# RWKV-6 attention and an MLP mixer on one core: the first channel weights' loads moved behind the third unit's last product, and their conversion moved with them

## The chip, the cores and the metric

The kernel runs on one core of one Trainium2 chip. The metric is the device time of one execution in microseconds. A core has TensorE (PE; its weight loads are listed as PEld), VectorE (DVE), ScalarE (ACT), GpSimd (POOL) and SyncE (SP), which here issues nearly all DMAs. Each engine takes its instructions in the order of its own queue.

## The reference, cut to what matters

Four batches, 8 heads, 768 tokens, 48 features a head (so 384 columns). First a linear attention with a decaying state, then a mixer over tokens and over channels:

```python
for t in range(S):
    cur = einsum('bhd,bhe->bhde', u * k[t], v[t])
    y[t] = einsum('bhd,bhde->bhe', r[t], state + cur)
    state = w[t][..., None] * state + einsum('bhd,bhe->bhde', k[t], v[t])
x = y.transpose(0, 2, 1, 3).reshape(B, S, H * D)
h = maximum(x.T @ w_tok1, 0) @ w_tok2        # per batch, 768 -> 256 -> 768
u = x + h.T
out = u + maximum(u @ w_ch1, 0) @ w_ch2      # 384 -> 1536 -> 384
```

The four weight matrices are 64-bit floats in HBM; all else is 32-bit.

## The kernel before, in words

The attention of a batch is cut into three *units* of 256 tokens, `e0`, `e1`, `e2` for the first batch. A unit loads its decays, keys and queries, and values (`load_w` L158, `load_part` L166 and `load_rk` L170, `load_v` L177), scans the decays on DVE (`ends`, `begins`), scales keys and queries, builds products of keys and queries (`own_gram`, `gram`, L308), carries the state over the chunks (`outer` L356, `scaled` L492, `update` L499), and forms its output in PSUM from two sets of products: `across` (L371, called by `before`) and `within` (L392, called by `after`). `taken` (L398) copies it into `x`, which is tiled as 128 tokens x 384 columns, six chunks a batch. `ranges` (L418) are ACT passes that check the decays' range.

The mixer of the first batch (`mixing`) begins with the *hidden* products over tokens (L883; twelve, `h[0]` to `h[11]`), `rectified` (ACT, L886, two), the *back* products (L891; six chunks), an addition into `x` on DVE (L893), and *turns*, transposes on TensorE (L902) that ACT copies into `xT` (L904). Then comes the up-projection over channels (L926, rectified by ACT at L929) and the down-projection (L937). One product of 32-bit floats is run as two passes, each with its weight load.

The weights reach 32 bits by conversions of 1,024 values a partition each, three for the token weights (`to_tok`) and nine for the channel weights (`to_ch`). `convert` (L230) makes for each one these functions, in the order in which they are named at the unpacking: a load of two DMAs of 512 KB (L257), `exponent` (x, DVE, L260), `mantissa` (m, DVE, L266), `raise_two` (p, ACT, L263), `add` (DVE, L272), `signs` (g, ACT, L269) and `put`, which is two things on DVE: the factor times its sign (L275), and the scaled product into the weights' tile (L278). The raw bits of `to_ch[0]` go to tile `z0`, those of `to_ch[1]` and `to_ch[2]` to parts of tile `raw`.

The order of the work around the change is written out by hand: the call of `strict` that begins at L1024 lists the pieces, and every engine, SP's DMA queue included, takes its instructions in this order (`strict`, L103). `behind(gate, f)` (L94) adds a wait, so that `f` is not issued before the last instruction of `gate` is done. From there on an order string (`WEAVES`) merges `first_mixing`, the attention of the next batch and the remaining conversions; its first pieces are the back products, the `put` of `to_ch[0]` and the steps of `to_ch[1]`. In the DVE queue after the list stand: L275 and L278 for `to_ch[0]`, L260 for `to_ch[1]`, the first L893, L266, two more L893, L272, two more L893, L275, L278. In the ACT queue after the list: L269 for `to_ch[1]`, two steps of the next unit's `own_u` (L324), L263 for `to_ch[1]`, and the copies L904.

SP's DMAs in this place, in order: values of the third unit, the first load of `to_ch[0]` (two DMAs into `z0`, behind `h[2]`), the load of `to_ch[2]` (behind `add1`), the load of `to_ch[1]` (behind `e2`'s `before`), keys and queries of unit 3 (four DMAs of 192 KB, behind `e0`'s `after`), those of unit 4 (four more), and the load of `to_ch[3]`.

Of the kernel before, what the change touches and what calls it, by code (L numbers as in the profile page):

```python
# [17 lines left out]
ALU = mybir.AluOpType  # L18
# [7 lines left out]
UB = C // UC  # L26
# [39 lines left out]
def rwkv6_then_mixer(  # L66
# [18 lines left out]
    pe, dve, act, pool, sp = nc.tensor, nc.vector, nc.scalar, nc.gpsimd, nc.sync  # L85
# [8 lines left out]
    def behind(gate, f):  # L94

        def g():
            done = len(block.instructions)
            f()
            tc.add_manual_dep(block.instructions[done], ended[gate], wait, reason="time of issue")

        return g
# [61 lines left out]
    def rk_of(i):  # L163
        return rks[i if i < UB else (i - UB) % 2]

    def load_part(i, n):  # L166
        for rows in (slice(0, 128),) if i < UB else (slice(0, D), slice(P, P + D)):
            sp.dma_start(rk_of(i)[rows, ts(n, COLS)], rk[i, n, rows, :])

    def load_rk(i):  # L170
        if i < NU:
            for n in (1, 0):
                load_part(i, n)
# [3 lines left out]
    def load_v(i):  # L177
        if i < NU:
            vs[i] = vpool.tile([128, UC, DM], f32, name="vt", tag=f"vt{i % 2 if i < UB else 1}")
            b, j = divmod(i, UB)  # L180
            sp.dma_start(vs[i], v[b, ts(j, UC * 128), :].rearrange("(c p) e -> p c e", p=128))
# [48 lines left out]
    def convert(pair, raw, room, signs_at=None):  # L230

        d64 = bits64[raw]
        lo, hi = (d64.rearrange("p (n two) -> p n two", two=2)[:, :, j] for j in range(2))
        top = d64.bitcast(u16).rearrange("p (n four) -> p n four", four=4)[:, :, 3]
        m, planes = mantissas[room], exponents[room]
        mf, e, power = m.bitcast(f32), *planes[:2]
        sign, factor = planes[2 * room].bitcast(bf16) if signs_at is None else signs_at, power.bitcast(bf16)

        (a, _), (b, _) = pair
        c, k = a.shape[1:]  # L240
        (row, _), (one, _) = a.ap[1:]
        apart = b.offset - a.offset if a.tensor is b.tensor else None
        beside = apart == k * one
        if beside:
            whole = bass.AP(a.tensor, a.offset, [list(a.ap[0]), [row, c], [one, 2 * k]])
        elif apart is not None and (c == 1 or apart == c * row):
            whole = bass.AP(a.tensor, a.offset, [list(a.ap[0]), [apart // c, 2 * c], [one, k]])
        else:
            whole = None

        def load():
            for n, (dst, src) in enumerate(pair):
                if beside:
                    to = d64.rearrange("p (c n k) -> p n c k", n=2, c=c)[:, n]
                else:
                    to = d64[:, ts(n, 2 * PIECE)].rearrange("p (c k) -> p c k", c=dst.shape[1])
                sp.dma_start(to, src)  # L257

        def exponent():
            dve.tensor_scalar(e, top, 0x7FF0, None, op0=ALU.bitwise_and)  # L260

        def raise_two():
            act.activation(power, e, AF.Relu, bias=rebias, scale=8.0)  # L263

        def mantissa():
            dve.tensor_scalar(m, hi, 0xFFFFF, 0x100000, op0=ALU.bitwise_and, op1=ALU.bitwise_or)  # L266

        def signs():
            act.activation(sign, hi.bitcast(i32), AF.Sign)  # L269

        def add():
            dve.scalar_tensor_tensor(mf, lo, 2.0 ** -32, m, op0=ALU.mult, op1=ALU.add)  # L272

        def put():
            dve.tensor_mul(factor, factor, sign)  # L275
            for dst, cols in [(whole, slice(0, 2 * PIECE))] if whole is not None else [(dst, ts(n, PIECE)) for n, (dst, _) in enumerate(pair)]:
                x, by = (t[:, cols].rearrange("p (c k) -> p c k", c=dst.shape[1]) for t in (mf, factor))
                dve.scalar_tensor_tensor(dst, x, 2.0 ** -20, by, op0=ALU.mult, op1=ALU.mult)  # L278

        return load, exponent, mantissa, raise_two, add, signs, put  # L280

    def blocks(t, src, c, k):
# [5 lines left out]
    def conversion(*weights, rooms):  # L288
        pieces = [e for w in weights for e in blocks(*w)]
        return [convert(pieces[2 * n:2 * n + 2], *rooms(n)) for n in range(len(pieces) // 2)]  # L290
# [9 lines left out]
    def put(q, j):  # L300
        return ts(j ^ q, T)
# [703 lines left out]
    def interleaved(order, *streams):  # L1005
# [7 lines left out]
    h = [lambda i=i, c=c: turned["hidden"](i, c) for c in range(C) for i in range(DTOK // 128)]  # L1013
    rectified = [lambda i=i: turned["rectified"](i) for i in range(DTOK // 128)]
    bits64.append(turned["xT"].rearrange("p m t -> p (m t)").bitcast(u32)[:, :4 * PIECE])
    to_tok = conversion((wtok1, w_tok1, 2, 256), (wtok2, w_tok2, 2, 256), rooms=lambda n: (3, 0) if n == 2 else (n, n))
    to_ch = conversion((now["wch1"], w_ch1, 1, 512), (now["wch2"], w_ch2, 4, 128), rooms=lambda n: (n % 2, 0, rks[2][:, ts(n % 2, PIECE)].bitcast(bf16)) if n else (2, 1))
    e0, e1, e2 = (unit(i) for i in range(UB))
    (_, x0, m0, p0, add0, g0, put0), (_, x1, m1, p1, add1, g1, put1), (_, x2, m2, p2, add2, g2, put2) = to_tok
    _, x3, m3, p3, add3, g3, _ = to_ch[0]  # L1020
    in_turn.update({pe.engine: None, dve.engine: None, act.engine: None, sp.engine: None})
    s0, s1, s2 = (e["updates"] for e in (e0, e1, e2))
    t0, t1, t2 = (e["scaled"] for e in (e0, e1, e2))
# [6 lines left out]
           behind(t0[2], to_tok[1][0]), e1["copied"][1], t1[0], e1["carry"], e2["own_u"][2], s1[0], g0, e0["seen"], e1["own_put"], e2["own_u"][3],  # L1030
           t1[1], e0["after"], e1["queries"], s1[1], e0["taken"][0], e2["ends"], m0, lambda: load_w(3), e1["gram"], lambda: load_v(2), e2["keys"],
           m1, t1[2], behind(e0["carry"], to_tok[2][0]), s1[2], add0, e2["tokens"], add1, e0["taken"][1], e0["taken"][2], t1[3], e2["copied"][0],
           e2["copied"][1], s1[3], t2[0], e1["ranges"][0], g1, put0, e1["before"], e2["carry"], behind(e1["before"], lambda: load_part(2, 0)), h[0],
           s2[0], h[1], e1["mask"], x2, e2["begins"], e1["seen"], e1["after"], t2[1], p2, e1["taken"][0], s2[1], e2["own_gram"], x1, e2["queries"],
           t2[2], lambda: load_v(UB), h[3], e1["taken"][1], s2[2], e1["taken"][2], t2[3], e2["own_put"], h[2], p1, e2["gram"], e2["before"], g2, m2,
           behind(h[2], to_ch[0][0]), h[4], e2["mask"], put1, e2["seen"], add2, e2["after"], e2["ranges"][0], e2["taken"][0], x3, h[5], h[6],
           e2["taken"][1], e2["taken"][2], h[7], h[8], e1["ranges"][1], h[9], g3, m3, behind(add1, to_ch[2][0]), h[10], h[11], rectified[0],
           rectified[1], p3, behind(e2["before"], to_ch[1][0]), behind(e0["after"], lambda: load_rk(3)), e2["ranges"][1], put2, add3)

    six_banks.close()  # L1040
    ps_g, ps_m = None, six_banks.enter_context(tc.tile_pool(name="ps_m", bufs=6, space=bass.MemoryType.PSUM))
# [228 lines left out]
```

## Time and profile before

| what | value |
|---|---|
| median of 3 runs | 486.51 us (485.17 to 490.95) |
| the profiled execution | 487.42 us |
| its span in the trace | 485.7 us |
| mean granted TensorE clock | 0.997 |
| PE, DVE, ACT busy | 464.4, 340.0, 254.0 us |

The span goes from the first instruction to the last; the time of the execution has 1.7 us more around it. A row of the timeline reads: start, duration, engine, line, operation, output<-input, shape, number of instructions, and in brackets the idle time before it with what ended it. "issue" there is idle time in which the engine waited for nothing that the profile shows.

### The profile page before, as it was taken

The numbers are of one execution on the slowest core, as the hardware profiler recorded it, in microseconds if no ns is written. First come the engines' busy times: TensorE is split into PE (matmuls) and PEld (weight loads), VectorE is DVE, ScalarE is ACT, GpSimd is POOL, SyncE is SP. The second block draws the span as 40 slices with busy tenths as digits, with TensorE's granted clock in tenths as the row PEclk, the third lists the DMA queues.
The fourth block names the chain that finished last, engine by engine and source line by source line (L and its number), as shares of the span: only waits on it lengthen the run. The fifth ranks groups of instructions, "written<-read, shape, count | busy, mean of one in ns | idle before, by whom it ended". The sixth has DMA issues, their size and how long they took to land.

```text
span 485.7 us, 12678 instructions
## 1 busy us (share of the span) xinstructions
PE 464.4 (96%) x5298; PEld 406.2 (84%) x5298; DVE 340.0 (70%) x478; ACT 254.0 (52%) x587; POOL 62.7 (13%) x58
## 2 busy tenths in 40 slices
PE   2897999999999999999999999999999999999995
PEld 2775588866697668999999979999999979999995
DVE  7999699697796788868855388758977365235331
ACT  5887666745678666453564336344646334134140
POOL 1000000000000000313232003040403003032030
PEclk9999999999999999999999999999999999999998
DMA  8868545690385495856636662385724622436321
GB/s 300 295 206 306 142 151 188 209 303 34 111 246 174 131 242 177 258 170 205 212 112 216 224 195 84 132 220 180 227 85 133 223 84 81 112 102 197 91 86 55
DMA packets 49407, 83.77 MB, mean 172 GB/s; under 512 B 4864, under 2 KB 40576, under 8 KB 49344
## 3 DMA queue, kind: packets, MB, share of 16 engines
q1 hardware_dynamic: 49056, 82.80, 54.4%
q8 instruction: 43, 0.70, 0.6%
q14 instruction: 20, 0.16, 0.1%
q10 hardware_dynamic: 288, 0.10, 0.1%
HBM read 71.87 MB, written 11.01 MB: 171 GB/s over the span
## 4 chain that ended last, share of the span: by engine, by line
PE 91%; DVE 2%; issue 1%; ACT 0%; DVEq 0%
PE h_ps L937 10%; PE ends_ps L730 8%; PE ends_ps L737 8%; PE ends_ps L732 8%; PE o_ps L748 8%; PE o_ps L750 8%; PE o_ps L749 8%; PE z_ps L926 7%; PE h_ps L653 5%; PE z_ps L922 3%; PE h_ps L684 3%; PE gram L308 3%; PE y_ps L392 2%; PE y_ps L371 2%; PE kv_ps L356 2%; PE h_ps L883 2%
## 5 line engine op out<-in xcount | busy, mean ns | idle before, releaser
L723 POOL TENSOR_TENSOR z_high<-z_high 128x384 fp32r<-128x384 f32 x48 | 61.4, 1289 | 406.5 <-ACT before L492 208.8
L756 DVE SCALAR_TENSOR_TENSOR x<-o_ps,x 128x384 f32<-128x384 f32 x35 | 19.1, 557 | 50.5 <-PE o_ps L750 50.5
L712 ACT ACTIVATE z_high<-ends_ps 128x384 fp32r<-128x384 f32 x48 | 23.5, 489 | 52.3 <-PE ends_ps L737 51.7
L730 PE MATMUL ends_ps<-x_forms,forms 128*128 128x384 f32 x216 | 50.4, 341 | 0.0
L737 PE MATMUL ends_ps<-z_more,forms 128*128 128x384 f32 x216 | 50.3, 341 | 0.0
L732 PE MATMUL ends_ps<-x_forms,ring 128*128 128x384 f32 x216 | 49.3, 337 | 0.0
L719 DVE SCALAR_TENSOR_TENSOR z_high<-ends_ps,z_high 128x384 fp32r<-128x384 f32 x48 | 26.5, 553 | 32.0 <-ACT z_high L712 31.9
L937 PE MATMUL h_ps<-wch,z 128*128 128x384 f32 x144 | 48.5, 490 | 0.0
L748 PE MATMUL o_ps<-forms,z_high 128*128 128x384 f32 x140 | 48.1, 343 | 0.0
L749 PE MATMUL o_ps<-ring,z_high 128*128 128x384 f32 x140 | 47.1, 337 | 0.0
L750 PE MATMUL o_ps<-forms,z_high 128*128 128x384 f32 x140 | 47.1, 336 | 0.0
L492 ACT ACTIVATE before<-state,to_end 112x48 f32<-112x48 f32 x132 | 33.2, 324 | 22.3 <-DVE state L507 21.4
L937 PEld LDWEIGHTS h_ps<-wch,z 128*128 128x128 f32 x144 | 26.7, 190 | 17.0
L737 PEld LDWEIGHTS ends_ps<-z_more,forms 128*128 128x128 f32 x216 | 39.0, 188 | 0.3 <-DVE z_more L625 0.2
L730 PEld LDWEIGHTS ends_ps<-x_forms,forms 128*128 128x128 f32 x216 | 38.0, 188 | 0.7
L732 PEld LDWEIGHTS ends_ps<-x_forms,ring 128*128 128x128 f32 x216 | 38.5, 188 | 0.0
L926 PE MATMUL z_ps<-xT,wch 128*128 128x256 f32 x144 | 32.2, 381 | 0.0
L926 PEld LDWEIGHTS z_ps<-xT,wch 128*128 128x128 f32 x144 | 26.9, 190 | 3.7
L715 ACT ACTIVATE z_high<-z_high 128x384 fp32r<-128x384 f32 x48 | 25.2, 525 | 3.3
L748 PEld LDWEIGHTS o_ps<-forms,z_high 128*128 128x128 f32 x140 | 26.3, 188 | 0.2
L749 PEld LDWEIGHTS o_ps<-ring,z_high 128*128 128x128 f32 x140 | 26.3, 188 | 0.0
L750 PEld LDWEIGHTS o_ps<-forms,z_high 128*128 128x128 f32 x140 | 26.3, 188 | 0.0
(194 smaller groups left out, 931.9 us busy)
## 6 DMA issues: line engine op xcount, KB each, us to landing
ring<-third SPq DMA_DIRECT2D x144, 192.0 KB, 3.2
raw<-in_w_ch_dram SPq DMA_DIRECT2D x16, 512.0 KB, 5.0
rk<-in_rk_dram SPq DMA_DIRECT2D x36, 192.0 KB, 5.9
near<-in_near_dram SPq DMA_DIRECT2D x8, 768.0 KB, 4.6
w<-in_w_dram SPq DMA_DIRECT2D x10, 520.5 KB, 3.6
vt<-in_v_dram SPq DMA_DIRECT2D x12, 384.0 KB, 4.3
out_dram<-x SPq DMA_DIRECT2D x17, 192.0 KB, 3.4
third<-forms SPq DMA_DIRECT2D x12, 192.0 KB, 3.4
```

The source lines that it names most:

```text
L492: act.mul(t[:ROWS, a], state[bt, g][:ROWS, a], by_last(c, j)[:, a:a + 1])
L715: act.mul(z_form(jt, 2), z_form(jt, 0).bitcast(f32), 1.0 / BASE)
L719: dve.scalar_tensor_tensor(z_form(jt, 1), a, 0.0, z_form(jt, 0).bitcast(f32), op0=ALU.max, op1=ALU.subtract)
L723: pool.tensor_add(z_form(jt, 2), z_form(jt, 2).bitcast(f32), z_form(jt, 1).bitcast(f32))
L730: pe.matmul(a, up[m], xf[0][:, m], start=m == 0, stop=False)
L732: pe.matmul(a, low[:, m], xf[1][:, m], start=False, stop=False)
L737: pe.matmul(banks["a", jt], joint, xf[2][:, m], start=False, stop=m == 2)
L748: pe.matmul(a, z[0], up, start=first, stop=False, skip_group_check=True)
L749: pe.matmul(a, z[1], held[bt, s, half, 1, jt], start=False, stop=False, skip_group_check=True)
L750: pe.matmul(a, z[2], joint, start=False, stop=last, skip_group_check=True)
L926: pe.matmul(ps, now["wch1"][:, m, ts(jt, 128)], xT[:, m, ts(s, SEG)], start=(m == 0), stop=(m == DM // 128 - 1))
L937: pe.matmul(ps, zs[s][:, jt, ts(n, 128)], now["wch2"][:, jt, :], start=(jt == 0), stop=(jt == NJ - 1))
```

## The change

`put` is cut in two, so that its halves can be listed separately; for the three token conversions they are named `product0` and `put0` and so on, and both stay on DVE. In the list, three things move:

- the load of `to_ch[0]` is issued behind `e2`'s `after` (the last product of the third unit) instead of behind `h[2]`. The loads of `to_ch[2]`, `to_ch[1]` and of unit 3's rows are listed behind it, in the same order and with their own gates as before;
- `x3`, `m3`, `g3`, `p3` (the first channel conversion's steps on DVE and ACT) move to the end of the list, ahead of `add3`;
- `product2` and `put2` thereby come ahead of `x3` on DVE, and `rectified` and the range check `e2["ranges"][1]` ahead of `g3` on ACT.

On DVE the only difference in order is that L260 and L266 of `to_ch[0]` come behind L275 and L278 of the third token conversion (L272 follows as before). On ACT L269 of `to_ch[0]`, which stood ahead of both L886, comes behind them and behind L418, with L263 next to it. The order on SP, TensorE and GpSimd is the same. Lines of the changed kernel are 5 to 7 higher from L281 on.

```diff
-        def put():
-            dve.tensor_mul(factor, factor, sign)
+        def signed(on=dve):
+            on.tensor_tensor(factor, factor, sign, ALU.mult)
+
+        def put(whole_step=True):
+            if whole_step:
+                signed()
...
+        put.apart = lambda on: (lambda: signed(on), lambda: put(False))
...
+    (product0, put0), (product1, put1), (product2, put2) = (put.apart(on) for put, on in zip((put0, put1, put2), (dve, dve, dve)))
...
-           e2["copied"][1], s1[3], t2[0], e1["ranges"][0], g1, put0, e1["before"], ...
+           e2["copied"][1], s1[3], t2[0], e1["ranges"][0], g1, product0, put0, e1["before"], ...
...
-           ..., e2["gram"], e2["before"], g2, m2,
-           behind(h[2], to_ch[0][0]), h[4], e2["mask"], put1, e2["seen"], add2, e2["after"], e2["ranges"][0], e2["taken"][0], x3, h[5], h[6],
-           e2["taken"][1], e2["taken"][2], h[7], h[8], e1["ranges"][1], h[9], g3, m3, behind(add1, to_ch[2][0]), h[10], h[11], rectified[0],
-           rectified[1], p3, behind(e2["before"], to_ch[1][0]), behind(e0["after"], lambda: load_rk(3)), e2["ranges"][1], put2, add3)
+           ..., e2["gram"], e2["before"], g2, m2, h[4], e2["mask"], product1, put1, e2["seen"], add2, e2["after"],
+           behind(e2["after"], to_ch[0][0]), e2["ranges"][0], e2["taken"][0], h[5], h[6], e2["taken"][1], behind(add1, to_ch[2][0]),
+           behind(e2["before"], to_ch[1][0]), behind(e0["after"], lambda: load_rk(3)), e2["taken"][2], h[7], h[8], e1["ranges"][1], h[9], h[10],
+           h[11], rectified[0], rectified[1], e2["ranges"][1], product2, put2, x3, m3, g3, p3, add3)
```

More of the change, by code (lines that the diff above doesn't have):

```diff
@@ L1032, in rwkv6_then_mixer @@
            m1, t1[2], behind(e0["carry"], to_tok[2][0]), s1[2], add0, e2["tokens"], add1, e0["taken"][1], e0["taken"][2], t1[3], e2["copied"][0],
-           e2["copied"][1], s1[3], t2[0], e1["ranges"][0], g1, put0, e1["before"], e2["carry"], behind(e1["before"], lambda: load_part(2, 0)), h[0],
-           s2[0], h[1], e1["mask"], x2, e2["begins"], e1["seen"], e1["after"], t2[1], p2, e1["taken"][0], s2[1], e2["own_gram"], x1, e2["queries"],
-           t2[2], lambda: load_v(UB), h[3], e1["taken"][1], s2[2], e1["taken"][2], t2[3], e2["own_put"], h[2], p1, e2["gram"], e2["before"], g2, m2,
-           behind(h[2], to_ch[0][0]), h[4], e2["mask"], put1, e2["seen"], add2, e2["after"], e2["ranges"][0], e2["taken"][0], x3, h[5], h[6],
-           e2["taken"][1], e2["taken"][2], h[7], h[8], e1["ranges"][1], h[9], g3, m3, behind(add1, to_ch[2][0]), h[10], h[11], rectified[0],
-           rectified[1], p3, behind(e2["before"], to_ch[1][0]), behind(e0["after"], lambda: load_rk(3)), e2["ranges"][1], put2, add3)
+           e2["copied"][1], s1[3], t2[0], e1["ranges"][0], g1, product0, put0, e1["before"], e2["carry"],
+           behind(e1["before"], lambda: load_part(2, 0)), h[0], s2[0], h[1], e1["mask"], x2, e2["begins"], e1["seen"], e1["after"], t2[1], p2,
+           e1["taken"][0], s2[1], e2["own_gram"], x1, e2["queries"], t2[2], lambda: load_v(UB), h[3], e1["taken"][1], s2[2], e1["taken"][2], t2[3],
+           e2["own_put"], h[2], p1, e2["gram"], e2["before"], g2, m2, h[4], e2["mask"], product1, put1, e2["seen"], add2, e2["after"],
+           behind(e2["after"], to_ch[0][0]), e2["ranges"][0], e2["taken"][0], h[5], h[6], e2["taken"][1], behind(add1, to_ch[2][0]),
+           behind(e2["before"], to_ch[1][0]), behind(e0["after"], lambda: load_rk(3)), e2["taken"][2], h[7], h[8], e1["ranges"][1], h[9], h[10],
+           h[11], rectified[0], rectified[1], e2["ranges"][1], product2, put2, x3, m3, g3, p3, add3)
     six_banks.close()
```

## The prediction, on record before the changed kernel ran

> **What bounds the kernel now.** I read the page first. TensorE is busy for 96% of the span and carries 91% of the chain that ended last.
>
> ```profile
> span 485.7 us, 12678 instructions
> PE 464.4 (96%) x5298; PEld 406.2 (84%) x5298; DVE 340.0 (70%) x478; ACT 254.0 (52%) x587; POOL 62.7 (13%) x58
> PE 91%; DVE 2%; issue 1%; ACT 0%; DVEq 0%
> ```
>
> Then the table by stage, for the place of the change (about 38 to 61 us) and for all that follows.
>
> ```profile
> 40.28:47.22 6.94, 4.21 (x127) 3.00 (x128) 6.87 (x10) 5.60 (x10) 0.00 (x0) 1.00 1.01 392
> 47.23:61.00 13.77, 13.19 (x48) 7.75 (x48) 8.99 (x13) 8.42 (x13) 0.00 (x0) 1.00 0.65 170
> 61.00:485.70 424.70, 418.97 (x4267) 372.60 (x4265) 287.54 (x418) 209.10 (x477) 61.39 (x48) 1.00 0.52 161
> ```
>
> The first pair of figures is the stretch and its length, then come busy time and instructions of PE, PEld, DVE, ACT, POOL, the granted clock, the DMA share and GB/s. From 61.0 on TensorE idles 424.70 - 418.97 = 5.7 us in all. So the moment at which it enters the first up-projection (L926) sets the end: a microsecond won or lost before 61.0 stays won or lost, as nothing later has slack to give back or take up.
>
> Third, the chain of waits in order of time (start, us, what) through that place.
>
> ```profile
> 39.72 0.56 issue
> ...
> 43.33 1.17 PE h_ps L883 x3
> 44.50 2.73 issue
> 47.23 3.72 PE h_ps L883 x11
> ...
> 50.98 0.50 ACT h L886
> ...
> 51.52 4.14 PE h_ps L891 x12
> 55.66 0.50 PE xT_ps L902 x3
> ...
> 61.01 1.08 PE z_ps L926 x5
> ```
>
> In the middle of the hidden products (L883) TensorE stands for 2.73 us on "issue": no semaphore ended it. By the table above, 127 products and 128 weight loads lie between this stop and the one at 39.72, 255 instructions; and the DMA view has the packets of the instruction queue (0.02 MB each). None is in flight in 40.3 to 44.9, when the data queue alone fills the DMA engines (first line); one fills 44.93 to 45.9 (second line: 6.3% of 16 engines over 0.97 us is one engine for all of it).
>
> ```profile
> q1 hardware_dynamic: 482, 1.78, 100.6%
> ...
> q8 instruction: 1, 0.02, 6.3%
> ```
>
> So the next block of TensorE's program, which I take to be asked for at 40.28 when the last began, came 4.65 us later, behind the weights' loads, and TensorE ran on 1.3 us after its end. This is what the change can remove. The TensorE that is released then meets a second limit, the DVE queue and its loads, which I read in the timelines of DVE, ACT, SP and PE.
>
> ```profile
> 43.95 0.69 DVE L260 TENSOR_SCALAR z<-z 128x1024 uint16<-128x1024 uint16 x1
> 45.88 1.22 DVE L278 SCALAR_TENSOR_TENSOR wtok<-raw 128x1024 f32<-128x1024 f32 x1
> 52.53 0.69 DVE L275 TENSOR_TENSOR z<-z 128x1024 bf16<-128x1024 bf16 x1 [4.30 <-ACT z L263]
> 53.26 1.22 DVE L278 SCALAR_TENSOR_TENSOR wch<-z 128x1024 f32<-128x1024 f32 x1
> 54.40 0.69 DVE L260 TENSOR_SCALAR raw<-raw 128x1024 uint16<-128x1024 uint16 x1
> 55.01 0.55 DVE L893 TENSOR_TENSOR x<-x,h_ps 128x384 f32<-128x384 f32 x1
> ```
>
> ```profile
> 46.04 1.11 ACT L269 ACTIVATE z<-z 128x1024 bf16<-128x1024 int32 x1
> 50.98 0.49 ACT L886 ACTIVATE h<-h_ps 128x384 f32<-128x384 f32 x1 [0.15 <-PE h_ps L883]
> 51.36 1.14 ACT L263 ACTIVATE z<-z,rebias 128x1024 uint16<-128x1024 uint16 x1
> 52.40 1.16 ACT L418 ACTIVATE junk<-first,most 112x1041 uint8<-112x1041 f32 x1
> 54.59 0.90 ACT L324 ACTIVATE near<-rk,u_col 112x256 f32<-112x256 f32 x2
> 56.43 0.46 ACT L904 COPY xT<-xT_ps 128x384 f32<-128x384 f32 x1
> ```
>
> ```profile
> 38.56 0.84 SPq L257 DMA_DIRECT2D z<-in_w_ch_dram  x2
> 39.50 2.81 SPq L257 DMA_DIRECT2D raw<-in_w_ch_dram  x4
> 42.36 10.00 SPq L168 DMA_DIRECT2D rk<-in_rk_dram  x8
> 58.28 21.53 SPq L257 DMA_DIRECT2D raw<-in_w_ch_dram  x8
> ```
>
> ```profile
> 42.18 1.15 PE L392 MATMUL y_ps<-vt,at 64*64 64x48 f32 x64
> ```
>
> Last, issues of single loads with the us to their landing: the two of the first load (38.56 and 38.95), the two that the second conversion needs (41.49 and 41.87), and the second half of unit 3's keys (42.84).
>
> ```profile
> z<-in_w_ch_dram SPq DMA_DIRECT2D x1, 512.0 KB, 3.7
> ...
> z<-in_w_ch_dram SPq DMA_DIRECT2D x1, 512.0 KB, 4.5
> ...
> raw<-in_w_ch_dram SPq DMA_DIRECT2D x1, 512.0 KB, 8.4
> ...
> raw<-in_w_ch_dram SPq DMA_DIRECT2D x1, 512.0 KB, 10.2
> ...
> rk<-in_rk_dram SPq DMA_DIRECT2D x1, 192.0 KB, 10.7
> ```
>
> They land at 42.3, 43.5, 49.9, 52.0 and 53.5. One row of SP's waits (total, times, longest) belongs to what stands behind them.
>
> ```profile
> SPq L257 <- DVE raw L272: 13.7, 2, 7.9
> ```
>
> **The change part by part.** Nothing is added or dropped; every piece is moved.
>
> *Splitting put* into signed product (L275) and scaled product (L278) leaves the first two conversions' instructions in place: 0.
>
> *The third put earlier.* Its two instructions pass two of the first channel conversion on DVE and start at 43.95 instead of 45.16, ending at 45.9 instead of 47.1. They feed the products of L891, which wait for ACT's L886 anyway: 0.
>
> *The loads later.* The first load's gate becomes the last product of L392, which ends at 42.18 + 1.15 = 43.33; it issues at 43.36 instead of 38.56, 4.80 us later. SP works in order, so the four loads of the second and third conversions and the eight of the units' rows go behind it, at about 44.3 to 45.9 and from 46.0. What stands behind them on SP, the load at 58.28, waits for DVE's L272 by the SP waits (below), and the eight are through at 42.36 + 10.00 + 4.80 = 57.2, so 1.1 us of cover are left. The first load lands at 43.5 + 4.8 = 48.3.
>
> *The stop.* With nothing in flight on the data queue from 40.3 to about 44.5, the block's fetch is no longer behind anything. Bounds: nothing is saved, or all it: the eleven products follow one another by 3.72 / 11 = 0.34 us, so the fourth was due at 43.33 + 3 x 0.34 = 44.35 and came at 47.23, 2.9 us late. I take 2.90, because a fetch that lasts 1 us and is used 1.3 us later fits easily into 40.28 to 44.35. The second L886 then starts at 50.98 - 2.90 = 48.08, TensorE starts L891 at 48.6 and is ready for the first turn (L902) at 52.75.
>
> [...]
>
> *The conversion begun later.* On DVE L260, L266 and L272 of the first conversion wait for its load: 48.35 to 50.75, where DVE sat idle before (4.30 us ahead of 52.53), so they fit. On ACT the signs (L269, at 46.04 before) now stand behind both L886 and the range check L418, in front of L263. So ACT goes L886 48.08, L418 48.47, signs 49.6, L263 50.7 to 51.8 (steps of 1.05 each, the spacing of such rows). DVE's L275 starts at 51.82 instead of 52.53: of 2.90 us saved, 2.2 go to two ACT steps set into the path, 0.7 remain. L278 follows, and DVE is at L260 of the *second* conversion at 53.70 instead of 54.40.
>
> *The second conversion's load.* That L260 stands in DVE's queue ahead of the first L893, for whose result the first turn waits. Before, its load had landed 2.4 us earlier (52.0 against 54.40), so it cost nothing; 4.80 us later this cover is gone. Upper bound: the same distance from the first load's landing, 52.0 - 43.5 = 8.5, so 56.8. Lower bound: the spacing of the first pair, 43.5 - 42.3 = 1.2 us a half-megabyte, so 48.3 + 4 x 1.25 = 53.3. The upper distance contains the fetch that held one of the 16 engines for 0.97 us, and whatever came of it; a load is complete with its last part. TensorE's next block is now asked for at 44.35, and 4.65 us of waiting would put it among the same loads. So I take a value in the upper half of the bounds, 55.4. DVE goes on at 55.45 instead of 54.40, L893 and the first turn follow with unchanged steps: +1.05 us. From there the row of products and turns to 61.0 is unchanged, and so is the shift.
>
> *The rows.* Unit 3's keys land at 53.5 + 4.8 = 58.3 at most, or 1.5 us behind the second conversion's load as before: 56.9. ACT's L324 (54.59 before) waits for them, then L263 and the copies of L904, the first two done by 59.9 (the first began at 56.43 before). L926 needs them at 61.01 + 1.05 = 62.1: still hidden, with 2.2 us to spare, and 2.3 at the upper bounds (61.1 against 63.4).
>
> Sum: -2.90 + 2.19 + 1.76 (DVE's new wait, 53.70 to 55.45) = +1.05 us. The profiled execution took 487.42 us (span 485.7 and 1.7 around it), 0.91 above the median of 486.51. So 488.5 by its own time, and 487.5 for the median.
>
> **The rivals.** *The loads land in time* (faster). If the moved loads come at the first pair's spacing, L260 finds its data before 53.70 and the 0.7 us of the ACT path are kept: 485.8. It decides at a landing of 54.40, past which it is a loss. For it: the fetch of 44.93 would not fall on the same loads. Against it: in the profile the later halves came 2.1 us apart, not 1.2 (49.9 and 52.0), and eight row loads now follow more closely.
>
> *The tail of the loads stays as slow as it was.* Landing at 56.8, DVE goes on at 56.85, +2.45: 489.0. For it: same loads in the same order. Against it: the fetch of 44.93 is no longer in the early part.
>
> *The stop stays.* If it isn't the loads that hold up the fetch, L886 stays at 50.98, ACT goes L418 51.36, signs 52.5, L263 53.6, DVE's L275 54.7 and L260 56.6: +2.2, 488.7. For it: the profile ties the stop to the fetch by time alone. Against it: the block's packet ran only when the queue had been full for 4 us. [...]
>
> A gain of the whole 2.90 us isn't among them: even with all loads in time, two ACT steps stand in the path.
>
> **How the numbers follow.** My forecast (landing 54.7 to 56.4, so +0.35 to +2.05; 486.9 to 488.6) has 0.45, loads in time 0.22, slow tail 0.18, the stop stays 0.12; 0.03 is left for a cascade that I don't see. The time is the likeliest one's, 487.5. The mechanisms reach from 485.8 to 489.0; the three runs of before scatter from 485.17 to 490.95, and a median of such runs by about 1 us, so the range is 484.8 to 490.0. Two per cent, about what a measurement of this kernel can tell from no change, is 9.7 us; no case reaches it. Faster 0.01, same 0.97, slower 0.02.
>
> **What would show it.** In the changed profile: no issue stop between 43.3 and 47, and the instruction queue's packet near 41; L886 near 47.4 and 48.1; ACT in the order L886, L418, L269, L263 without gaps; DVE idle before the first L260 until 48.3, and again before the second L260, ended by a DMA, with TensorE idle ahead of the first L902 until about 56.6. I am wrong if DVE doesn't wait there, if the stop stays, if ACT holds up L926 through L324, or if idle time of TensorE after 61 departs from 5.7 us by more than 1 us.

## The result, and the profile after

| | before | changed |
|---|---|---|
| median, us (17 runs each, same chip) | 486.51 (485.06 to 491.56) | 492.37 (489.69 to 498.4) |
| ratio, 95% interval | | 1.011 (1.0077 to 1.0144) |
| profiled execution: span, us | 485.7 | 494.6 |
| third unit's last product (L392, now L397) ends at | 43.33 | 48.35 |
| from there to the first turn (L902, now L907) | 12.28 | 14.43 |
| from there to the first up-projection (L926, now L931) | 17.52 | 22.10 |
| from there to the end of the span | 442.37 | 446.21 |

The changed kernel is 1.1% slower, some 5.4 us (1.1% of 486.5) with an interval of 3.7 to 7.0. That is within 2%, as forecast, but 4.9 us over the forecast of 487.5 and above the range, which ended at 490.0. One of the 17 runs of the changed kernel and three of the 12 of the kernel "both" (below) fell in a slow state; the nine others of "both" have a median of 490.01 us, 0.3% over the 488.57 of kernel before beside them.

The two profiled spans differ by 8.9 us, more than the timed runs do. 48.35 - 43.33 = 5.0 us of it lie ahead of the third unit's last product, where the change moves no product and, of the loads, only takes away those that kernel before has started by then. One and the same kernel varies there as much: this product ended at 43.33, 46.61 and 46.03 in three executions of kernel before and at 48.35 and 42.13 in two of the changed one, and between 42.12 and 48.83 over all the executions profiled for this study. So I compare executions from this product on, and give times after it as "+8.19". Kernel before was profiled three times (442.37, 441.03 and 441.88 from this product to the end, mean 441.8), the changed kernel twice (446.21, 446.45, mean 446.3): 4.6 us longer, inside the timed interval. At the first up-projection the difference is larger, +22.2 against +17.0 in the means of the same executions; 0.5 to 0.7 us of it come back at the very end: from the start of TensorE's last product to the end of the span it takes 5.36 us in the changed kernel's two profiles and 5.89 to 6.07 in kernel before's.

Three rows of the page of the changed kernel:

```profile
span 494.6 us, 12678 instructions
PE 471.9 (95%) x5298; PEld 411.9 (83%) x5298; DVE 340.5 (69%) x478; ACT 254.5 (51%) x587; POOL 62.6 (13%) x58
PE 94%; DMA 3%; SPq 1%; issue 1%; ACT 0%; DVE 0%; DVEq 0%
```

TensorE does the same 5298 products in 7.5 us more of busy time (471.9 against 464.4). About 3 us of that lie ahead of the change, in a stretch at half clock (from 33.6 to 40.4, below); the rest says that part of the loss is not waiting. DMA, which the old line doesn't name, now has 3% of the chain. The chain of waits through the place (start, us, what):

```profile
51.02 10.46 DMA raw<-in_w_ch_dram
...
61.57 0.70 DVE raw L260
62.26 0.47 DVE x L898
62.78 0.90 PE xT_ps L907 x3
63.68 2.56 PE h_ps L896 x4
```

Where the old chain had a stop on "issue" and then TensorE's own products, this one has a load of 10.46 us, DVE's first step on it (L260), the addition behind that in DVE's queue (L898), and only then the first turn. TensorE's timeline (start, us, line, tiles, count, and in brackets the idle before with what ended it):

```profile
48.29 4.78 PE L888 MATMUL h_ps<-x,wtok 128*128 128x384 f32 x14
53.65 4.14 PE L896 MATMUL h_ps<-h,wtok 128*128 128x384 f32 x12 [0.58 <-ACT h L891]
62.78 0.90 PE L907 MATMUL xT_ps<-ident,x 128*128 128x128 f32 x3 [4.99 <-DVE x L898]
```

The fourteen hidden products now run in one row: the stop of 2.73 us is gone, and L896 starts at 53.65 - 48.35 = +5.30 instead of +8.19, 2.89 us earlier. But then TensorE stands for 4.99 us, and the three products of the first turn take 0.90 us where they took 0.50. The table by stage (stretch, length, busy time of PE, PEld, DVE, ACT, POOL, granted clock, DMA share, GB/s) says why:

```profile
48.40:57.80 9.40, 8.81 (x26) 4.66 (x26) 6.78 (x9) 6.91 (x11) 0.00 (x0) 1.00 0.90 340
57.80:62.70 4.90, 0.00 (x0) 0.00 (x0) 2.16 (x4) 1.14 (x1) 0.00 (x0) 0.82 1.04 236
60.90:67.70 6.80, 4.92 (x12) 3.26 (x13) 4.38 (x7) 3.92 (x6) 0.00 (x0) 0.50 0.69 161
74.00:489.00 415.00, 415.00 (x4249) 369.41 (x4248) 283.54 (x411) 207.28 (x474) 61.35 (x48) 1.00 0.52 163
```

The clock granted to TensorE is 1.00 up to the idle stretch, falls to 0.50 at 60.9, some 3.1 us into it, stays there for 6.8 us and comes back at 67.7. The 4.92 us of products at half speed cost half of that, 2.46 us. From the first turn to the up-projection it takes 22.10 - 14.43 = 7.67 us instead of 17.52 - 12.28 = 5.24: 2.43 us more. From 74 to its last products TensorE has no idle time at all, so it wins nothing back.

DVE's timeline shows who made it wait:

```profile
54.22 0.69 DVE L260 TENSOR_SCALAR z<-z 128x1024 uint16<-128x1024 uint16 x1 [2.42 <-DMA z<-in_w_ch_dram]
...
56.87 0.69 DVE L275 TENSOR_TENSOR z<-z 128x1024 bf16<-128x1024 bf16 x1
57.60 1.23 DVE L282 SCALAR_TENSOR_TENSOR wch<-z 128x1024 f32<-128x1024 f32 x1
61.57 0.70 DVE L260 TENSOR_SCALAR raw<-raw 128x1024 uint16<-128x1024 uint16 x1 [2.74 <-DMA raw<-in_w_ch_dram]
62.17 0.55 DVE L898 TENSOR_TENSOR x<-x,h_ps 128x384 f32<-128x384 f32 x1
```

The first conversion goes through without a gap at the end. DVE is ready for the second conversion at +10.5 (61.57 - 2.74 - 48.35), its load is complete at +13.12, and the addition for the first turn stands behind. ACT's timeline:

```profile
53.10 0.49 ACT L891 ACTIVATE h<-h_ps 128x384 f32<-128x384 f32 x1 [0.15 <-PE h_ps L888]
53.49 1.16 ACT L423 ACTIVATE junk<-first,most 112x1041 uint8<-112x1041 f32 x1
54.64 1.16 ACT L269 ACTIVATE z<-z 128x1024 bf16<-128x1024 int32 x1
55.71 1.13 ACT L263 ACTIVATE z<-z,rebias 128x1024 uint16<-128x1024 uint16 x1
```

This is the forecast order, L891, range check, signs, L263, without gaps: the two ACT steps did enter the path.

### The profile page after: what moved, and what is told of

It reads as the page before. It is cut to its first block, busy times and chain, and to the rows that moved or that the text cites. A ratio compares the mean times of both kernels' runs of the same rounds, so it can differ in the third digit from the quotient of the medians.

```text
span 494.6 us, 12678 instructions
## 1 busy us (share of the span) xinstructions
PE 471.9 (95%) x5298; PEld 411.9 (83%) x5298; DVE 340.5 (69%) x478; ACT 254.5 (51%) x587; POOL 62.6 (13%) x58
## 4 chain that ended last, share of the span: by engine, by line
PE 94%; DMA 3%; SPq 1%; issue 1%; ACT 0%; DVE 0%; DVEq 0%
PE h_ps L942 10%; PE ends_ps L735 8%; PE ends_ps L742 8%; PE ends_ps L737 8%; PE o_ps L753 8%; PE o_ps L755 7%; PE o_ps L754 7%; PE z_ps L931 6%; PE h_ps L658 5%; PE gram L313 4%; PE kv_ps L361 3%; PE y_ps L397 3%; PE z_ps L927 3%; PE y_ps L376 3%; PE h_ps L689 3%; DMA raw<-in_w_ch_dram 2%
## 5 line engine op out<-in xcount | busy, mean ns | idle before, releaser
L931 PE MATMUL z_ps<-xT,wch 128*128 128x256 f32 x144 | 32.2, 381 | 0.0
L931 PEld LDWEIGHTS z_ps<-xT,wch 128*128 128x128 f32 x144 | 26.9, 190 | 3.7
```

Of the source, the lines that this page charges most:

```text
L931: pe.matmul(ps, now["wch1"][:, m, ts(jt, 128)], xT[:, m, ts(s, SEG)], start=(m == 0), stop=(m == DM // 128 - 1))
```

## The experiments

My theory after the result: the change removes the stop (-2.9 us) and pays for it in three pieces: the two ACT steps set into the path, DVE's new wait for the second conversion's load, and TensorE's clock, which the resulting idle of 5 us breaks (+2.4 us). Rivals: the order alone or the late loads alone cost the time; the rows' loads, not the second conversion's, are what is late; the slow stretch after the first turn is something other than the clock. "First turn" and the like are again counted from the third unit's last product.

| kernel | timed median, us | ratio to before, 95% | L896 starts | first turn | up-projection | to the end |
|---|---|---|---|---|---|---|
| loads alone | 494.27 | 1.0101 (1.0052 to 1.015) | 7.36 | 14.16 | 19.41 | 443.72 |
| order alone | 492.6 | 1.0068 (1.0028 to 1.0107) | 7.14 | 13.39 | 18.63 | 443.20 |
| second load first | 490.98 | 1.005 (1.0014 to 1.0087) | 5.29 | 11.57 | 17.87 | 443.11 |
| kept busy | 491.29 | 1.0056 (1.0016 to 1.0096) | 5.29 | 14.42 | 19.66 | 444.07 |
| additions first | 490.42 | 1.0034 (0.9998 to 1.0069) | 5.29 | 9.26 | 16.37 | 442.21 |
| rows before the third load | 490.12 | 1.0037 (0.9997 to 1.0077) | 5.29 | 11.58 | 16.83 | 442.13 |
| both | 491.22 | 1.0058 (1.0018 to 1.0097) | 5.30 | 9.27 | 14.46 | 441.62 |
| changed, again | 493.0 | 1.012 (1.0062 to 1.0178) | 5.30 | 14.27 | 22.36 | 446.45 |
| third behind the turns | 487.65 | 0.9968 (0.9929 to 1.0006) | 5.29 | 9.27 | 14.45 | 439.12 |
| earlier gate | 487.2 | 0.9972 (0.9932 to 1.0012) | 5.29 | 9.26 | 14.45 | 438.87 |

**The loads alone.** On the kernel before, only the gate of the first load is moved; conversions keep their order.

```diff
-           behind(h[2], to_ch[0][0]), h[4], e2["mask"], put1, e2["seen"], add2, e2["after"], e2["ranges"][0],
+           h[4], e2["mask"], put1, e2["seen"], add2, e2["after"], behind(e2["after"], to_ch[0][0]), e2["ranges"][0],
```

> Only the loads move (first load behind the third unit's last product); the conversion's place in the list stays as before. Measure: from the end of the third unit's last product (L392 before) to the start of the first up-projection (L926 before): 17.7 us before, 22.2 us in the changed kernel's profile. Theory A (the second conversion's load lands late, DVE's queue holds the first addition behind it, TensorE idles 5.0 us and its clock is then granted at half): the second load lands some 13.0 us after the first is issued, the first turn comes 2 us late again, but TensorE reaches it later, as the third put now waits for the first load (idle in two pieces of about 3.6 and 2 us in place of one of 5.0). If the clock holds 19.7 us, if the 3.6 us break it up to 22.2. In both, no issue stop in the hidden products. Rival B (the conversion begun later is what costs, not the loads): 17.7 us or less.

TensorE's timeline of this kernel:

```profile
48.76 4.78 PE L883 MATMUL h_ps<-x,wtok 128*128 128x384 f32 x14
56.19 4.14 PE L891 MATMUL h_ps<-h,wtok 128*128 128x384 f32 x12 [2.65 <-ACT h L886]
62.99 0.55 PE L902 MATMUL xT_ps<-ident,x 128*128 128x128 f32 x3 [2.67 <-DVE x L893]
```

The stop is gone here as well (x14 in one row), so the late loads alone take it away. What was 4.99 us of idle is cut in two, 2.65 us for L886, which now stands behind ACT's signs, and 2.67 us ahead of the turn; in this execution the clock held (the four products behind the turn take 1.46 us). In others it may not have: the mean granted clock of the ten timed runs is 0.9905 against 0.9938 of kernel before's beside them, and they lose 4.9 us where this profile loses 2. The first turn, at +14.16, is only 0.1 to 0.3 us earlier than in the changed kernel's two profiles. So the landing sets the turn, in whichever order the conversion stands.

**The order alone.** On the changed kernel, the loads go back to their old place.

```diff
-           ..., g2, m2, h[4], ..., e2["after"], behind(e2["after"], to_ch[0][0]), e2["ranges"][0],
+           ..., g2, m2, behind(h[2], to_ch[0][0]), h[4], ..., e2["after"], e2["ranges"][0],
```

> Only the list's order of the conversion changes; the first load keeps its early gate. Theory A: the issue stop of 2.7 us in the hidden products stays, the two ACT steps ahead of L263 delay DVE's L275 by 2.2 us, so the first turn comes 2.2 us late, TensorE idles about 2.2 us ahead of it, too short for half clock: 19.9 us for the measure (17.7 before, 22.2 changed), +2.2 us in the time. Rival B (the order costs it all): 22.2 us, +5 us in the time. If the loads do not cause the stop: no stop here, and 17.0 us.

```profile
49.06 3.71 PE L888 MATMUL h_ps<-x,wtok 128*128 128x384 f32 x11 [1.69 <-issue]
...
59.60 0.55 PE L907 MATMUL xT_ps<-ident,x 128*128 128x128 f32 x3 [2.11 <-DVE x L898]
```

TensorE's timeline has the stop on "issue" again, in front of the same eleven products. With early loads it is there, with late ones not. With a stop of 2.73 us kernel before had its first turn at +12.28, so with one of 1.69 it would be 11.24. This kernel has it at 13.39: the order by itself costs 2.15 us, against the 2.2 that I had put for two ACT steps. The idle of 2.11 us cost no clock: the four products behind the turn take 1.46 us.

**Kernel before, two profiles more.** The unchanged kernel, profiled again to see whether the stop belongs to one execution.

> The kernel before once more, for a second trace: is the issue stop in the hidden products the same in each execution? If the fetch stands behind the loads' packets, there is a stop of 1.5 to 3 us at the same place; from the third unit's last product to the end 441 to 442.5 us. If the stop of the first profile was an accident: none, 439.5 us.

> The kernel before a third time; as the second look: a stop of 1.5 to 3 us in the hidden products, or none if the first was an accident. Also how far the time up to the third unit's last product, which no kernel here changes, varies from one execution to the next.

The chains of waits, first of the second profile, then of the third:

```profile
47.78 1.59 issue
```

```profile
47.19 2.40 issue
```

The stop is always there, at the same place, but its length is 2.73, 1.59 and 2.40 us, 2.24 in the mean. It is there in all four profiles with early loads (these three and the order alone) and in none of the ten with late ones (the other nine kernels of the table and the changed kernel's first profile). So the loads ahead of it cause it.

The DMA view ties this to the fetch of instructions, by the time of one packet in the row of the instruction queue. Here is this row for 47.08 to 48.10 in kernel before's second profile, and for 46.26 to 47.24 in the changed kernel:

```profile
q8 instruction: 1, 0.02, 6.2%
...
q8 instruction: 1, 0.02, 6.1%
```

Each is the one packet in question, and fills one of the 16 engines for about 1 us. In the four profiles with early loads it begins 0.43 to 1.60 us after the third unit's last product, 3.3 to 4.7 us after the start of the block before it (the seventh of the 64 products of L371), and TensorE goes on 1.27 to 1.45 us after its end. In the ten with late loads it begins 1.56 to 2.20 us ahead of that product, 0.7 to 1.4 us after the block's start, and TensorE doesn't stop.

**The second conversion's load first.** The loads of the second and third conversion change places on SP.

```diff
-           behind(add1, to_ch[2][0]), behind(e2["before"], to_ch[1][0]),
+           behind(e2["before"], to_ch[1][0]), behind(add1, to_ch[2][0]),
```

> The changed kernel with the loads of the second and third channel conversions exchanged on the DMA queue. Theory A: the second conversion's load lands some 8.9 us after the first is issued instead of 13.0, DVE goes on at the ACT path's time, the first turn comes 0.8 us earlier than before, TensorE idles 2.1 us instead of 5.0, the clock stays full: 16.9 us for the measure (17.7 before, 22.2 changed), time about 0.8 us under before's and 5 to 6 under the changed kernel's. Rival B (order of the conversion): no gain over the changed kernel. Rival C (the rows of the next unit hold ACT): no gain either, since they land as late as now.

TensorE's timeline, then ACT's:

```profile
55.52 0.55 PE L907 MATMUL xT_ps<-ident,x 128*128 128x128 f32 x3 [2.14 <-DVE x L898]
...
61.82 1.13 PE L931 MATMUL z_ps<-xT,wch 128*128 128x256 f32 x4 [0.89 <-ACT xT L909]
```

```profile
59.08 0.91 ACT L329 ACTIVATE near<-rk,u_col 112x256 f32<-112x256 f32 x2 [4.75 <-DMA rk<-in_rk_dram]
```

The first turn comes at +11.57, 0.7 us before kernel before's 12.28, where 0.8 was expected: it did wait for this load and no other. The idle is 2.14 us, and the clock stays whole (1.46 us for the four products behind the turn). The up-projection missed its 16.9 by 1 us for a reason that I had not put in: ACT stands 4.75 us for unit 3's keys (L329), and the copies of the turns (L909) stand behind it. With the first wait shortened, the rows' loads are the next to be late. The time missed too: 0.8 us under kernel before's was expected, and the timed runs are 0.5% (2.4 us) over it.

**Kept busy.** On the changed kernel, seven calls of products that nobody reads (x14 in the trace) are put ahead of the first turn, so that TensorE has work in the idle time. They change nothing in the output.

```diff
+            if rounded and c == 0:
+                warm = bank("warm")[:, :DM]
+                for i in range(7):
+                    pe.matmul(warm, now["wtok2"][:, 0, ts(0, 128)], h1[:, 0, :], start=True, stop=True)
```

> The changed kernel with seven products more (L891's shape, into a bank that nothing reads, about 4.5 us) ahead of the first turn, where TensorE idles 5.0 us. Nothing else is moved. Theory A with the clock as its second half: the half-rate stretch of 6.8 us goes, the turns and products after it keep their full pace, and although TensorE has more to do the measure falls by 2.4 us, from 22.2 to about 19.8, the time by as much. If the half clock has another cause or costs nothing: 22.2 us or more.

TensorE's timeline and the table by stage:

```profile
53.21 4.68 PE L908 MATMUL warm<-h,wtok 128*128 128x384 f32 x14
58.36 0.55 PE L911 MATMUL xT_ps<-ident,x 128*128 128x128 f32 x3 [0.47 <-DVE x L898]
58.74 1.46 PE L896 MATMUL h_ps<-h,wtok 128*128 128x384 f32 x4
```

```profile
53.40:60.00 6.60, 6.13 (x21) 3.38 (x21) 3.85 (x7) 2.21 (x4) 0.00 (x0) 1.00 1.00 223
```

The first turn is no sooner, +14.42 against 14.43, as DVE waits as before. But the clock stays at 1.00, the first four products behind the turn take 1.46 us in the timeline, where the changed kernel's take 2.77, and the up-projection starts at +19.66 instead of 22.10. So 2.44 us of the loss is the clock, and by the profiles products added to the kernel make it faster. The timed runs point the same way: the mean granted clock is 0.9893 over the changed kernel's 17 runs and 0.994 over this kernel's 10, which is what kernel before has (0.993 to 0.994 in 23 to 31 runs). The step in the clock, 0.005, is 2.3 us of 490. The ratios to kernel before, 1.0056 here and 1.011 for the changed kernel, differ in the same direction, but their intervals overlap.

**The changed kernel again.**

> The changed kernel once more beside the others on one chip, to compare them with it. Theory A: idle of about 5 us before the first turn and half clock after it in this execution too, 22 us for the measure; without the half clock it would be 19.6.

```profile
56.39 0.90 PE L907 MATMUL xT_ps<-ident,x 128*128 128x128 f32 x3 [4.84 <-DVE x L898]
57.09 2.77 PE L896 MATMUL h_ps<-h,wtok 128*128 128x384 f32 x4
```

TensorE's timeline shows the long idle and the half speed again, 4.84 us and 2.77 us for four products.

**The additions first.** DVE's additions for the first turns go ahead of the second conversion, by the string that weaves conversion steps (4) with pieces of the back products and turns (0) and of unit 3 (1).

```diff
-    "444011144004000400440400000104...
+    "004440044040011144040400000104...
```

> The changed kernel with only the DVE and ACT queues rearranged behind the list: the first two additions of the back products stand ahead of the first conversion's put, and the first turns' copies ahead of the rows' scaling; all loads stay where the change put them. Measure as before, from the end of the third unit's last product to the first up-projection: 17.5 us before, 22.1 changed. Theory A (a late load costs only through what is queued behind it): the first turn comes at about 9.5 us after that product instead of 14.4, TensorE never idles 3 us at a stretch, full clock, 16 to 17 us for the measure; time 0.5 to 1.5 us under before's. Rival (the late load itself is what the up-projection waits for): 19.5 us or more.

```profile
63.09 0.55 PE L907 MATMUL xT_ps<-ident,x 128*128 128x128 f32 x3 [1.70 <-DVE x L898]
```

In TensorE's timeline the wait of 4.99 us ahead of the first turn is gone, the first turn at +9.26. But the third turn stands 1.70 us for its addition: the string puts two additions ahead of the second conversion, and the third is still behind it in DVE's queue. After its first four products the up-projection, which starts at +16.37, stands another 1.27 us for a copy by ACT. In the timed runs the expected gain of 0.5 to 1.5 us did not come: they are 0.3% over kernel before's.

**The rows before the third load,** with the second conversion's load first.

```diff
-           behind(add1, to_ch[2][0]), behind(e2["before"], to_ch[1][0]), behind(e0["after"], lambda: load_rk(3)),
+           behind(e2["before"], to_ch[1][0]), behind(e0["after"], lambda: load_rk(3)), behind(add1, to_ch[2][0]),
```

> The changed kernel with the DMA order second conversion, unit 3's rows, third conversion. In the run with second and third exchanged the first turn came at 11.6 us as expected, but ACT then stood 4.8 us for the rows, ahead of the turns' copies. Theory A with this second wait: rows land by about 11 us after the product instead of 14.3, the first turn stays at 11.6, the up-projection starts at 16.8 instead of 17.9 (17.5 before); time 0.7 us under before's. If ACT's wait is no cause: 17.9 us again.

The up-projection starts at +16.83 as expected (16.8), 1 us before that of the kernel with the second load first. That confirms that the rows' loads held it up there. The timed runs again miss the expected gain (0.7 us): they are 0.4% over kernel before's, with an interval that includes 1.

**Both** edits together.

> Both of the two: queues rearranged and DMA order second conversion, rows, third conversion. Theory A: nothing late is ahead of TensorE any more, the first turn comes at about 9.5 us and the up-projection at 14.7 to 15.5 us (17.5 before), 2 to 2.9 us under before's time, the whole of the issue stop that went. If some limit that I have not seen remains: 16.5 us or more.

TensorE's timeline, then ACT's:

```profile
61.29 8.90 PE L931 MATMUL z_ps<-xT,wch 128*128 128x256 f32 x40 [2.75 <-ACT xT L909]
```

```profile
59.74 1.13 ACT L269 ACTIVATE first<-raw 128x1024 bf16<-128x1024 int32 x1 [2.16 <-DMA raw<-in_w_ch_dram]
60.78 0.46 ACT L909 COPY xT<-xT_ps 128x384 f32<-128x384 f32 x1
```

The up-projection starts at +14.46, a little before the 14.7 to 15.5 that were expected, and after its first four products TensorE stands for 2.75 us: the fourth turn's copy is behind the third conversion's signs on ACT, and these wait for the load that was put last. Three times the same pattern: one wait removed, the next queue's load is late. To the end it is 441.62 us, as kernel before, and the timed runs show none of the 2 to 2.9 us that were expected.

**The third conversion behind the turns.** As both, with the third conversion's steps woven in later.

```diff
-    "004440044040011144040400000104...
+    "004440044040011144000440000104...
```

> The version with both rearrangements, and the signs and exponent of the third conversion listed behind the fourth turn as well: in the run before, its up-projection began at 14.5 us after the third unit's last product, as expected, but stood 2.75 us a moment later, as ACT held the fourth turn's copy behind the signs that waited for the third conversion's load. Theory A: this wait goes too, at most 0.6 us are left for the second conversion's put; from that product to the end of the span 440.0 us (442.4 in the profile of before, 446.2 changed, 441.6 with both). If the time is bounded elsewhere: 441.6 again.

```profile
48.43 4.78 PE L888 MATMUL h_ps<-x,wtok 128*128 128x384 f32 x14
...
57.77 0.49 PE L907 MATMUL xT_ps<-ident,x 128*128 128x128 f32 x3
...
62.95 3.30 PE L931 MATMUL z_ps<-xT,wch 128*128 128x256 f32 x13
```

In TensorE's timeline no stop, no wait for a turn, none after the up-projection's start. From the last product to the end it is 439.12 us, 2.7 under kernel before's mean, about the size of the whole stop (1.59 to 2.73). The timed ratio is 0.9968, with an interval that includes 1, so the timed runs by themselves do not show a gain.

**An earlier gate.** The same with the first load's gate one step sooner.

```diff
-           behind(e2["after"], to_ch[0][0]),
+           behind(e2["before"], to_ch[0][0]),
```

> The same, with the first load behind the third unit's product with the state (L371 before) instead of its last product: about 1.9 us earlier, still behind the fetch that follows the block's start. Theory A: no issue stop comes back, the loads land 1.9 us earlier, and the distance to the end is the 440.0 us of the version beside it or up to 0.6 us less. If the early loads bring the stop back, up to 2.7 us more.

No stop came back, and nothing was won: 438.87 us to the end, ratio 0.9972. The gate itself is not what limits this version.

## Why the prediction was wrong

- *What bounds the kernel* held. TensorE idles 0 us from 74 to 489, and 5.0 us in all behind the start of the up-projection (5.7 before). The change lives or dies ahead of the up-projection.
- *The stop* held: the profiles with early and late loads tie it to them, and the packet forecast near 41 (-2.3 from the third unit's last product) came at -2.08. That -2.90 met -2.89 to the hundredth is luck: the first profile of kernel before had the longest stop of three, and against their mean (L896 at +7.69) the gain is 2.4 us. The rival that the stop stays is refuted.
- *The conversion begun later* held: ACT's order is the forecast one, and DVE is ready for the second conversion at +10.48 (58.83 - 48.35) against 53.70 - 43.33 = +10.37. The first load was later than forecast, though: DVE begins on it at +5.87 (54.22 - 48.35), not at +5.02, and had just enough cover.
- *The second conversion's load* was mis-sized. I took a landing of 55.4, which is 55.4 - 43.33 = +12.07; it came at +13.12, and at +12.97 in the second profile. That is 1.1 us later, near the upper bound (+13.5), the rival of the slow tail. A fetch does fall among these loads, as the prediction allowed: the next packet of the instruction queue begins at 54.27, which is +5.9, and lasts 1.04 us. The value between the two bounds was a choice that no row fixed, and it was too early. So the first turn came 14.43 - 12.28 = 2.15 us later, not 1.05.
- *"From there the row of products and turns to 61.0 is unchanged"* is the step that failed. It holds in instructions and not in time. I had TensorE ready for the first turn at 52.75 and the turn at about 56.6, so the idle of 3.9 us stands in the prediction, but priced only as delay. At the 4.99 us that it became, it also halved the clock for 6.8 us: +2.43. The sum had no term for the clock, and neither had any rival, so the range ended too low. With the two corrections the sum is +1.05 + 1.10 + 2.43 = +4.58, which is the shift of the up-projection, 22.10 - 17.52, against the first profile; against the mean of the three it is 5.2, as their mean stop is shorter.
- *The clock* was left out. In the profile of before the longest idle of TensorE in this place, the stop of 2.73 us, left it at 1.00; what a wait of 3.9 us does to it no row there showed, so a case with half clock had to stand in the range. The idles of 4.99 and 4.84 us were each followed by 0.50.
- *The rows* held: the copies of L909 came in time for the up-projection, which follows the last turn without a wait. The cover lasts only while the first wait is there: with the second load first, ACT stands 4.75 us on L329.
- *The median.* Profiled spans cannot be set against the median to a microsecond: 5.0 of the 8.9 us between the two lie before the change.

Two things stay open. The kernels "additions first", "rows before the third load" and "both" are timed slower than kernel before (by 0.3 to 0.4%, for "both" in nine of its twelve runs), while their single profiles, from the last product to the end, are within 0.5 us of its mean. For "rows before the third load" part of that is the clock: its 12 timed runs have a mean of 0.9908 against 0.9928 of kernel before's on the same chip, 1 us of 488. For those nine of "both" it is 0.9918, half a microsecond, and for "additions first" 0.9927, nothing. What remains was not traced. And when the clock is halved (below) is known in part only.

## What to carry to other kernels

Price an idle stretch of TensorE twice: as delay, and as clock. Here single idles of up to 2.75 us in this place cost no clock in the traces, and those of 4.84 and 4.99 us did; in between nothing was measured. Where the clock may fall, add half of the busy time of the products that follow at half speed, and put such a case into the range. When loads are moved later, follow each engine's queue to the first instruction that waits for each of them, in the order of landing: here the second load, the rows and the third load became the limit one after the other, and a profile as much shorter as the stop is long came out only when all three were cleared.

## What the runs showed of the hardware

- The clock falls 3.1 us into the idle of 4.99 us and 3.8 us into that of 4.84, and comes back 6.8 us later. But length alone doesn't decide. Idles of 2.73 us (kernel before), 2.75 (both) and 2.65 followed by 2.67 (loads alone) left the clock at 1.00, while early in the changed kernel a shorter one did not. TensorE's timeline:

```profile
34.26 1.74 PE L361 MATMUL kv_ps<-vt,kT 64*48 64x48 f32 x43 [1.90 <-issue]
```

The table by stage around it, and for the stretch ahead of the later fall:

```profile
30.19:33.60 3.41, 1.97 (x72) 1.48 (x72) 3.11 (x4) 3.41 (x10) 0.00 (x0) 1.00 0.72 220
33.70:40.30 6.60, 6.04 (x81) 4.23 (x84) 3.51 (x3) 2.39 (x7) 0.00 (x0) 0.50 0.18 66
57.50:60.91 3.41, 0.29 (x1) 0.00 (x0) 1.29 (x2) 0.00 (x0) 0.00 (x0) 1.00 1.05 250
```

An idle of 1.90 us, and 0.50 for 6.8 us from within it.

- In the changed kernel's trace the clock changes at 33.60, 40.43, 60.91 and 67.74 us, so after 6.83, 20.48 and 6.83, which are 2, 6 and 2 times 3.41. What sets these lengths was not shown. In the 3.41 us ahead of the two falls before the first turn TensorE was busy for 8% and for none of the time (first and second profile). Ahead of the early fall it was busy for 58%, mostly with products 48 and 64 wide, and in the 3.41 us up to the end of kernel before's stop, 43.82 to 47.23, for 0.68 us, which is 20%, and there the clock stayed at 1.00. So the busy share of the last 3.41 us does not tell by itself when the clock falls; what does was not found. Such early stretches, in ten of the 14 traces (mean granted clock from 30 to 50 us 0.91 in kernel before's second profile, 0.83 in "third behind the turns"), are a part of why the third unit's last product ends anywhere from 42.12 to 48.83 us.

- A stop of TensorE on "issue" comes and goes with the loads that are in flight: 1.59 to 2.73 us in four profiles with half-megabyte loads ahead of it, none in ten with these loads started 2 to 5 us later. It is tied to the fetch of instructions by the time of its packet in all 14 traces: begun 3.3 to 4.7 us after the block's start in the four, 0.7 to 1.4 in the ten. Why the packet comes so late behind the loads was not found.
